# A fused retention and two-layer kernel on one core: plain outputs for units 5 to 7 and an earlier first block

## The chip, the core and the metric

The kernel runs on one core of a Trainium2 chip. A core has a matrix engine, TensorE (PE in the profile; PEld is its loading of stationary operands), and three engines that work on tiles: VectorE (DVE), ScalarE (ACT) and GpSimd (POOL). SyncE (SP) issues transfers; ACT and POOL can issue them too. Each engine works off its own instructions in the order in which they were written, and waits for the others through semaphores. The metric is the time of one execution on the device in microseconds (us); the kernel before takes 290.12 us, the median of 4 runs (289.74 to 290.54).

## What is computed

A retention layer (attention without a softmax, with a causal decay for each head) over 8 batches of 576 tokens, 8 heads of 64, and then two dense layers with a leaky rectifier between them on all 4608 tokens. Inputs and output are float32.

```python
scores = q @ k^T / sqrt(64)                          # per batch and head
gamma  = 1 - 2 ** (-5 - head)
ret    = scores * where(i >= j, gamma ** (i - j), 0)
x      = (ret @ v), heads side by side               # 4608 x 512
h      = x @ w_in                                    # 512 x 2048
g      = maximum(0.01 * h, h)
out    = g @ w_out                                   # 2048 x 512
```

## The kernel before

**Units and groups.** The tokens are cut into 36 units of 128, each of two chunks of 64, and into 9 groups of four units (512 tokens). Retention is done chunk by chunk with a running state, so a unit needs the state of the one before it. Units 0 to 3 make group 0, units 4 to 7 group 1.

**A unit's steps.** `load` brings k, q and v, 256 KB each. `cast_k` (ACT), `cast_q` and `cast_v` (L175, L179) make float16 copies, the latter two with a decay factor. q and k are transposed: in the beginning on PE (`turn_act`, `turn`: four matmuls into a PSUM tile and a copy to the tile qkT, L207), from unit 8 on by a transfer on the SP queue (`transpose_dma`, L183). `scores` (L218, L227) makes the products of q and k and the new state terms in one PSUM tile. `masks` (L236) applies the causal mask on DVE, `state` (L258 to L264) adds up the state on DVE, and `state_cast` (L279) gives it in float16.

**Two forms of a unit's outputs.** The part from inside the chunk (mask times v) and the part from the state have to be summed. `outputs` (L294, L305) writes the two parts to separate halves of a PSUM tile: 32 matmuls. Then `own` (L361) copies one half to SBUF on ACT, and `add` (L366) adds the other half to it on DVE, which gives the unit's columns of xT, the first layer's input. `finish2` is these three. `outputs_acc` (L327, L339) sums in PSUM: two rounds of 16 matmuls with a drain of PE between them; then ACT alone copies the sum to xT (`x_copy`, L347). `finish` is `outputs_acc`, `x_copy` and the cast of the unit's second state. `first_outputs` is the same form in another PSUM pool.

**First layer.** `h_half(g, a, fb)` does half a group's tokens (two units) for 256 of the 2048 columns: 8 matmuls 128x256 (L379), then the leaky rectifier on ACT (L393). `h_unit(u, fb)` does one unit's tokens for 512 columns in 16 matmuls 128x128. `h_block` does a whole group for 128 columns. A block needs the xT of its tokens and the quarter of w_in that holds its columns. All first-layer blocks, PE transposes and fillers take turns in the four PSUM tiles named acc. `keep_warm(n)` issues n matmuls on a tile of zeros whose result nobody reads.

**Second layer.** Group 0 uses plain products (`wide`, L429, 16 groups of four matmuls). The later groups use a scheme of seven block products instead of eight (`seven`, L493); it needs differences of blocks of w_out, made once on DVE (`mix_weights`, L454), and sums of blocks of g (`mix`, L473).

**The order.** Nothing is scheduled: the order on every engine is that of the program's lines. Lines 600 to 646 do units 0 to 3 with fillers between; lines 716 to 784 do units 4 to 7 between blocks of the first layer of groups 0 and 1; the loop at line 799 does the second layer of group 0, with `burst(u)` (scores, and the outputs of the unit before) of unit 8 after the fifth and of unit 9 after the tenth piece. Loads of units 0 to 7 and the weights go out on POOL's queue, save three at the start. The loads of units 8 to 10 and then the transposes of units 8 and 9 stand in that order on SP's queue; the first of these loads waits for the third of four w_out transfers (L762).

Of the kernel before, what the change touches and what calls it, by code (L numbers as in the profile page):

```python
# [18 lines left out]
def kernel(  # L19
# [9 lines left out]
    nc = tc.nc  # L29
# [54 lines left out]
    def behind(dma, *others):  # L84
        for o in others:
            tc.add_manual_dep(
                dma.ins,
                o.ins.name,
                mybir.DependencyInfo(
                    mybir.DependencyClass.Sync, mybir.DependencyReason.DATA  # L90
                ),
                reason="order of loads",
            )
# [20 lines left out]
    def half(i):  # L114
        return slice(CH * i, CH * i + CH)
# [3 lines left out]
    def load(u, eng=None, after=None):  # L119
        for x in (1, 0, 2):  # L120
            t = ld_pool.tile([P, H, D], FP, name=f"t32_{x}")
            t32[u, x] = t
            c = 2 * u
            same = c % CB + 1 < CB
            e = eng[x] if isinstance(eng, dict) else eng or nc.sync
            engs = e if isinstance(e, tuple) else (e,)
            n = H // len(engs)
            for j, rows in ((0, P),) if same else ((0, CH), (1, CH)):
                b, w = (c + j) // CB, (c + j) % CB
                for i, e in enumerate(engs):  # L130
                    hs = slice(n * i, n * i + n)
                    d = e.dma_start(
                        out=t[CH * j : CH * j + rows, hs],
                        in_=(q, k, v)[x][b, hs, CH * w : CH * w + rows, :].rearrange(
                            "h t d -> t h d"
                        ),
                    )
                    if after is not None and (x in after or not isinstance(after, dict)):
                        behind(d, *(after[x] if isinstance(after, dict) else after))
                        after = None  # L140
                    last_load[u, x] = d
# [24 lines left out]
    def decay(u, x):  # L166
        w = kinds.index((place(2 * u), place(2 * u + 1)))
        return tab_sb[:, w, x, :].unsqueeze(2).to_broadcast([P, H, D])
# [5 lines left out]
    def cast_q(u, eng):  # L174
        eng.tensor_tensor(out=qk16[u][:, 0], in0=t32[u, 0], in1=decay(u, 0), op=MUL)  # L175

    def cast_v(u, eng):
        v16[u] = a_pool.tile([P, H, D], F16, name="v16")
        eng.tensor_tensor(out=v16[u], in0=t32[u, 2], in1=decay(u, 1), op=MUL)  # L179
# [54 lines left out]
    def masks(u):  # L234
        s16s[u] = b_pool.tile([P, 2, NP, CH], F16, name="s16")
        nc.vector.tensor_tensor(  # L236
            out=s16s[u],
            in0=sc_tiles[u][:, :, 0],
            in1=mask_sb.unsqueeze(1).unsqueeze(1).to_broadcast([P, 2, NP, CH]),
            op=MUL,  # L240
        )
# [28 lines left out]
    def live(u, j):  # L270
        return (2 * u + j) % CB != CB - 1

    def state_cast(u, copy, js=(0, 1)):
        js = [j for j in js if live(u, j)]
        if len(js) == 2:
            copy(out=st16[u], in_=s32s[u])  # L276
        else:
            for j in js:
                copy(out=st16[u][:, j], in_=s32s[u][:, j])  # L279

    def st_before(u, j):
        if (2 * u + j) % CB == 0:
            return zst
        return st16[u][:, 0] if j else st16[u - 1][:, 1]

    def outputs(u):
        ot = ot_pool.tile([P, 2, 2 * NP, CH], FP, name="ot")
        ot_tiles[u] = ot
        far = ot[:, :, NP : 2 * NP].rearrange("q g (c j) t -> q g c j t", j=2)
        for c in range(NP):  # L290
            for j in range(2):
                for o in range(2):
                    h = c + NP * o
                    nc.tensor.matmul(  # L294
                        out=ot[half(o), j, c, :],
                        lhsT=v16[u][half(j), h, :],
                        rhs=s16s[u][half(j), h % 2, h // 2, :],
                        start=True, stop=True, skip_group_check=True,
                    )
        for j in range(2):  # L300
            for c2 in range(NP // 2):
                for o in range(2):
                    for g in range(2):
                        h = 2 * c2 + g + NP * o
                        nc.tensor.matmul(  # L305
                            out=far[half(o), g, c2, j, :],
                            lhsT=st_before(u, j)[half(g), h // 2, :],
                            rhs=qkT[u][half(g), 0, h // 2, half(j)],
                            start=True, stop=True, skip_group_check=True,
                        )  # L310
# [40 lines left out]
    def x_of(u):  # L351
        g, t0 = u // 4, (u % 4) * P
        if g not in xT:
            xT[g] = x_pool.tile([P, NP, TOK], F16, name="xT")
        return xT[g][:, :, t0 : t0 + P]
# [3 lines left out]
    def own(u):  # L359
        owns[u] = b_pool.tile([P, NP, 2, CH], FP, name="own")  # L360
        nc.scalar.copy(  # L361
            out=owns[u], in_=ot_tiles[u][:, :, 0:NP].rearrange("q j c t -> q c j t")
        )

    def add(u):
        nc.vector.tensor_tensor(  # L366
            out=x_of(u).rearrange("q (c g) t -> q c g t", g=2),
            in0=ot_tiles[u][:, :, NP : 2 * NP].rearrange("q g (c j) t -> q c g (j t)", j=2),
            in1=owns[u].rearrange("q (c g) j t -> q c g (j t)", g=2),
            op=ADD,  # L370
        )
# [5 lines left out]
    def h_mm(hps, n, g, f, ts):  # L377
        for c in range(NP):
            nc.tensor.matmul(  # L379
                out=hps[:, n, :],  # L380
                lhsT=w_in16[:, c, f * P : (f + 1) * P],
                rhs=xT[g][:, c, ts],
                start=(c == 0),
                stop=(c == NP - 1),
            )

    def g_tile(g):
        if g not in g_t:
            g_t[g] = g_pool.tile([P, NF, TOK], F16, name="gt")
        return g_t[g]  # L390

    def leaky(out, in_):
        nc.scalar.activation(out=out, in_=in_, func=mybir.ActivationFunctionType.Lrelu)  # L393
# [6 lines left out]
    def h_half(g, a, fb):  # L400
        ts = slice(a * HT, (a + 1) * HT)
        hps = acc_pool.tile([P, 2, HT], FP, name="acc")
        for n in range(2):
            h_mm(hps, n, g, 2 * fb + n, ts)
        leaky(g_tile(g)[:, 2 * fb : 2 * fb + 2, ts], hps)

    def h_unit(u, fb):
        g, t0 = u // 4, (u % 4) * P
        ts = slice(t0, t0 + P)
        hps = acc_pool.tile([P, 4, P], FP, name="acc")  # L410
        for n in range(4):
            h_mm(hps, n, g, 4 * fb + n, ts)
        leaky(g_tile(g)[:, 4 * fb : 4 * fb + 4, ts], hps)
# [142 lines left out]
    def keep_warm(n):  # L556
        t = acc_pool.tile([P, 1, TOK], FP, name="acc")
        for _ in range(n):
            nc.tensor.matmul(out=t[:, 0, :], lhsT=idle[:, 0:P], rhs=idle, start=True, stop=True)
# [6 lines left out]
    pool_copy, act_copy, dve_copy = nc.gpsimd.tensor_copy, nc.scalar.copy, nc.vector.tensor_copy  # L566
# [17 lines left out]
    def turn_act(u, x):  # L584
        transpose_pe(u, x)
        transposed(u, x, act_copy)
# [49 lines left out]
    cast_q(3, nc.vector)  # L636
    cast_v(3, nc.vector)
    turn_act(3, 0)
    keep_warm(2)
    masks(2)  # L640
    scores(3)
    state_last(2)
# [6 lines left out]
    def halves(g, *items):  # L649
        for a, fb in items:  # L650
            h_half(g, a, fb)

    def cast_qv(u):
        cast_q(u, nc.vector)
        cast_v(u, nc.vector)

    def turn(u, x):
        transpose_pe(u, x)
        transposed(u, x, dve_copy)

    def settle(u):
        state(u, 0)
        state_cast(u, dve_copy, (0,))
        masks(u)
        state(u, 1)

    def finish(u):
        outputs_acc(u)
        x_copy(u)
        state_cast(u, act_copy, (1,))  # L670

    def finish2(u):
        outputs(u)
        own(u)
        add(u)
# [37 lines left out]
        ahead(u + 2)  # L713


    halves(0, (0, 0), (0, 1))
    finish2(3)
    state_cast(3, act_copy, (1,))
    halves(0, (0, 2), (0, 3))
# [19 lines left out]
    scores(5)  # L739
    settle(5)  # L740
    cast_k(6)
    cast_qv(6)
    halves(0, (0, 6), (0, 7))
    finish(5)
    halves(0, (1, 6))
    turn(6, 1)
    cast_k(7)
    halves(0, (1, 7))
    turn(6, 0)
    cast_qv(7)  # L750
    h_unit(5, 0)
    scores(6)
    settle(6)
    h_unit(5, 1)
    turn(7, 1)
    halves(1, (0, 4))
    finish(6)
    turn(7, 0)
    halves(1, (0, 5))
    scores(7)  # L760
    settle(7)
    load(8, after=(w_out_loads[2],))  # L762
    load(9)
    halves(1, (0, 6), (0, 7))
    h_unit(6, 0)
    finish(7)
    h_unit(6, 1)
    mix_weights(0, 0)
    mix_weights(0, 1)
    h_unit(7, 0)  # L770
# [83 lines left out]
```

## Time and profile before

| what | value |
|---|---|
| median of 4 runs | 290.12 us (289.74 to 290.54) |
| profiled execution, its own time | 290.54 us |
| its span, first to last instruction | 288.8 us |
| busy time PE, DVE, ACT, POOL | 280.8, 170.1, 144.5, 103.6 us |
| granted clock of TensorE, mean | 1.000 |
| mean length of a DVE sum (L366), an ACT own copy (L361) | 682 ns, 586 ns |

The span is what the profile shows, and 1.7 us of the execution lie outside it. The stretch of the profile that the change touches runs from 16 to some 50 us. Times of instructions are given from the start of the span. A line of the timeline gives the start, the length, the engine, the line of the program, the operation, what it writes and reads, the shapes, the number of instructions merged in it, and in brackets how long its engine was idle ahead of it and what ended that. A matmul's end is modelled: the next one starts well before the end of the last.

### The profile page before, as it was taken

To read this page: it belongs to the slowest core of one execution; us is meant where nothing else is said; L and a number is where in the kernel's file an instruction comes from. 1 tells how busy PE (TensorE), PEld (TensorE's weight loads), DVE (VectorE), ACT (ScalarE), POOL (GpSimd) and SP (SyncE) were. 2 spreads that over 40 slices of the span, in tenths; PEclk is the share of its full clock that TensorE was granted. 3 is DMA by queue.
4 is the path that set the end of the run, shared out by engine and by line. 5 is a ranking of instruction groups with operands and counts; after the bars stand their busy time and mean duration, and the time that the engine had idled before them with its cause. 6 is when DMAs were issued, how large, how long until landed. Compare 5 with 4: busy or idle time off the path is not lost.

```text
span 288.8 us, 9437 instructions
## 1 busy us (share of the span) xinstructions
PE 280.8 (97%) x4113; PEld 191.6 (66%) x4113; DVE 170.1 (59%) x294; ACT 144.5 (50%) x254; POOL 103.6 (36%) x124
## 2 busy tenths in 40 slices
PE   8799999999999999999999999999999999999994
PEld 2468888645874587458745874587458844884584
DVE  2875668774663595359545863586268636840352
ACT  3766766633337732773277327731773176307610
POOL 8969502645433324332424333234225413000000
PEclk9999999999999999999999999999999999999999
DMA  8999999999999999966796669766986151012003
GB/s 218 295 231 203 289 207 205 192 176 223 176 255 278 226 205 223 265 147 148 176 260 152 148 148 288 149 147 150 279 162 147 42 179 39 5 62 86 0 2 145
DMA packets 131738, 50.01 MB, mean 173 GB/s; under 512 B 121264, under 2 KB 126000, under 8 KB 131696
## 3 DMA queue, kind: packets, MB, share of 16 engines
q1 hardware_dynamic: 125392, 39.59, 59.1%
q0 software_dynamic: 6016, 9.70, 15.1%
q8 instruction: 32, 0.52, 0.8%
q10 hardware_dynamic: 288, 0.11, 0.1%
q14 instruction: 10, 0.08, 0.1%
HBM read 36.81 MB, written 9.44 MB: 160 GB/s over the span
## 4 chain that ended last, share of the span: by engine, by line
PE 91%; DVE 4%; DMA 2%; issue 1%; ACT 1%; POOL 0%; DVEq 0%; POOLq 0%
PE acc L379 43%; PE acc L493 34%; PE acc L429 5%; PE sc L218 3%; DMA t<-in_q_dram 2%; PE ot L294 1%; PE sc L227 1%; PE ot L305 1%; PE acc L200 1%; DVE qk L175 1%; DVE s L236 1%; PE ot L327 1%; DVE st L279 1%; DVE s L260 1%; DVE v L179 0%
## 5 line engine op out<-in xcount | busy, mean ns | idle before, releaser
L379 PE MATMUL acc<-xT,w_in 128*128 128x512 f16 (+2 forms) x768 | 130.9, 326 | 0.0
L393 ACT ACTIVATE gt<-acc 128x512 f16<-128x512 f32 x144 | 85.9, 598 | 56.2 <-PE acc L379 54.5
L379 PEld LDWEIGHTS <-w_in 128*128 128x128 f16 x768 | 68.1, 98 | 51.3
L493 PEld LDWEIGHTS <-gt 128*128 128x128 f16 x640 | 61.8, 98 | 9.1
L236 DVE TENSOR_TENSOR s<-sc,cs 128x512 f16<-128x512 f32 x34 | 23.3, 685 | 40.0 <-PE sc L227 40.0
L493 PE MATMUL acc<-w_out,gt 128*128 128x256 f16 x384 | 45.9, 273 | 0.2
L276 POOL CAST st<-s 128x512 f16<-128x512 f32 x21 | 12.8, 611 | 89.7 <-DVE s L260 56.3
L361 ACT COPY own<-ot 128x512 f32<-128x512 f32 x30 | 17.6, 586 | 42.6 <-PE ot L305 34.4
L175 POOL TENSOR_TENSOR qk<-t,cs 128x512 f16<-128x512 f32 x28 | 30.0, 1071 | 19.8 <-ACT xT L347 15.2
L473 DVE TENSOR_TENSOR mix<-gt 128x1024 f16<-128x1024 f16 x16 | 14.8, 923 | 30.6 <-ACT gt L393 30.6
L179 POOL TENSOR_TENSOR v<-t,cs 128x512 f16<-128x512 f32 x28 | 31.3, 1117 | 1.7 <-DMA t<-in_v_dram 1.7
L493 PE MATMUL acc<-w_mix,gt 128*128 128x256 f16 x256 | 30.6, 273 | 0.0
L493 PE MATMUL acc<-w_mix,mix 128*128 128x256 f16 x256 | 29.6, 273 | 0.0
L493 PEld LDWEIGHTS <-mix 128*128 128x128 f16 x256 | 25.0, 98 | 3.1 <-DVE mix L473 0.2
L172 ACT CAST qk<-t 128x512 f16<-128x512 f32 x36 | 22.3, 620 | 5.8 <-DMA t<-in_k_dram 3.8
L366 DVE TENSOR_TENSOR xT<-ot,own 128x512 f16<-128x512 f32 x30 | 20.5, 682 | 3.8 <-ACT own L361 3.8
L260 DVE TENSOR_TENSOR s<-sc,s 128x256 f32<-128x256 f32 x37 | 15.5, 419 | 2.4 <-PE sc L227 1.7
L218 PEld LDWEIGHTS <-qkT 64*64 64x64 f16 x576 | 7.9, 107 | 12.4 <-issue 10.5
L519 DVE TENSOR_TENSOR osb<-acc,u 128x512 f32<-128x512 f32 (+1 forms) x17 | 11.2, 656 | 8.0 <-PE acc L493 8.0
L473 DVE TENSOR_TENSOR mix<-mix,gt 128x1024 f16<-128x1024 f16 x16 | 14.8, 932 | 0.5
L429 PE MATMUL acc<-w_out,gt 128*128 128x512 f16 x64 | 14.3, 379 | 0.0
L279 POOL CAST st<-s 128x256 f16<-128x256 f32 x7 | 3.2, 455 | 31.0 <-DVE s L264 19.1
(60 smaller groups left out, 240.0 us busy)
## 6 DMA issues: line engine op xcount, KB each, us to landing
out_dram<-osb SPq DMA_DIRECT2D x17, 512.0 KB, 4.0
t<-in_k_dram SPq DMA_DIRECT2D x27, 256.0 KB, 3.9
t<-in_q_dram SPq DMA_DIRECT2D x26, 256.0 KB, 4.4
t<-in_v_dram SPq DMA_DIRECT2D x25, 256.0 KB, 4.7
w_in<-in_moe_w_in_dram POOLq DMA_DIRECT2D x8, 256.0 KB, 6.9
w_out<-in_moe_w_out_dram POOLq DMA_DIRECT2D x4, 512.0 KB, 10.5
t<-in_v_dram POOLq DMA_DIRECT2D x7, 256.0 KB, 5.5
t<-in_q_dram POOLq DMA_DIRECT2D x6, 256.0 KB, 5.8
```

The source lines that it names most:

```text
L172: nc.scalar.copy(out=qk16[u][:, 1], in_=t32[u, 1])
L175: eng.tensor_tensor(out=qk16[u][:, 0], in0=t32[u, 0], in1=decay(u, 0), op=MUL)
L179: eng.tensor_tensor(out=v16[u], in0=t32[u, 2], in1=decay(u, 1), op=MUL)
L236: nc.vector.tensor_tensor(out=s16s[u], in0=sc_tiles[u][:, :, 0], in1=mask_sb.unsqueeze(1).unsqueeze(1).to_broadcast([P, 2, NP, CH]), op=MUL,)
L260: nc.vector.tensor_tensor(out=to, in0=st, in1=carry[0], op=ADD)
L361: nc.scalar.copy(out=owns[u], in_=ot_tiles[u][:, :, 0:NP].rearrange("q j c t -> q c j t"))
L366: nc.vector.tensor_tensor(out=x_of(u).rearrange("q (c g) t -> q c g t", g=2), in0=ot_tiles[u][:, :, NP : 2 * NP].rearrange("q g (c j) t -> ...
L379: nc.tensor.matmul(out=hps[:, n, :], lhsT=w_in16[:, c, f * P : (f + 1) * P], rhs=xT[g][:, c, ts], start=(c == 0), stop=(c == NP - 1),)
L393: nc.scalar.activation(out=out, in_=in_, func=mybir.ActivationFunctionType.Lrelu)
L429: nc.tensor.matmul(out=ys[tb], lhsT=g_t[0][:, f, tb * P : (tb + 1) * P], rhs=w_out16[:, f, :], start=(f == 0), stop=(f == NF - 1),)
L473: nc.vector.tensor_tensor(out=z[:, fs], in0=a[:, fs], in1=b[:, fs], op=op)
L493: nc.tensor.matmul(out=r[name][tb][:, 0, :] if apart else r[name][0][:, tb, :], lhsT=lhs[:, f, tb * P : (tb + 1) * P], rhs=rhs[:, f, :], s ...
```

## The change

- The first block of the first layer, `h_half(0, 0, 0)`, is issued where two fillers stood, between the q transpose of unit 3 and unit 2's masks, and is taken out of its old place ahead of unit 3's outputs. These therefore come one block sooner.
- Units 5, 6 and 7 use the plain outputs with the sum on DVE, where they had the form that sums in PSUM.
- For unit 5, the cast of v of unit 6 goes behind the sum. For unit 6, the casts of q and v of unit 7 go behind unit 6's masks and states, and the sum goes behind the q transpose's copy of unit 7. For unit 7, the outputs go behind both of unit 6's first-layer blocks, and two blocks of group 1 that stood ahead go behind unit 7's outputs.

```diff
@@ -636,7 +636,7 @@
     turn_act(3, 0)
-    keep_warm(2)
+    h_half(0, 0, 0)
     masks(2)
...
-    halves(0, (0, 0), (0, 1))
+    halves(0, (0, 1))
     finish2(3)
...
     cast_k(6)
-    cast_qv(6)
+    cast_q(6, nc.vector)
     halves(0, (0, 6), (0, 7))
-    finish(5)
+    finish2(5)
+    cast_v(6, nc.vector)
+    state_cast(5, act_copy, (1,))
     halves(0, (1, 6))
     turn(6, 1)
     cast_k(7)
     halves(0, (1, 7))
     turn(6, 0)
-    cast_qv(7)
     h_unit(5, 0)
     scores(6)
     settle(6)
+    cast_qv(7)
     h_unit(5, 1)
     turn(7, 1)
     halves(1, (0, 4))
-    finish(6)
+    outputs(6)
+    own(6)
     turn(7, 0)
+    add(6)
+    state_cast(6, act_copy, (1,))
     halves(1, (0, 5))
     scores(7)
     settle(7)
     load(8, after=(w_out_loads[2],))
     load(9)
+    h_unit(6, 0)
+    h_unit(6, 1)
+    finish2(7)
+    state_cast(7, act_copy, (1,))
     halves(1, (0, 6), (0, 7))
-    h_unit(6, 0)
-    finish(7)
-    h_unit(6, 1)
     mix_weights(0, 0)
```

No function is added or altered; both forms of the outputs stand in the kernel before.

## The prediction

> **What bounds the kernel now.** I read the page first, then the chain of work that ended last, then the timeline of each engine from 16 to 60 us, the DMA issues of that stretch, and the waits.
>
> ```profile
> PE 280.8 (97%) x4113; PEld 191.6 (66%) x4113; DVE 170.1 (59%) x294; ACT 144.5 (50%) x254; POOL 103.6 (36%) x124
> ...
> PE 91%; DVE 4%; DMA 2%; issue 1%; ACT 1%; POOL 0%; DVEq 0%; POOLq 0%
> ```
>
> TensorE (PE) is busy 97% of the span and makes 91% of the chain, so a microsecond taken from PE shows at the end only if nothing later makes PE wait for it. The change ends at about 49 us. What lies next on PE is in the chain (start, length, work):
>
> ```profile
> 48.26 6.28 PE acc L379 x80
> 54.54 4.32 PE acc L429 x20
> 58.86 0.25 PE sc L218 x16
> ```
>
> First-layer blocks, 20 matmuls of the second layer, then the scores of unit 8, with no gap. The timeline of the SP queue (start, length of the issue) and of PE around that place:
>
> ```profile
> 43.74 0.37 SPq L132 DMA_DIRECT2D t<-in_k_dram  x1
> ...
> 53.70 0.73 SPq L132 DMA_DIRECT2D t<-in_v_dram  x1
> 54.61 3.37 SPq L183 DMA_TRANSPOSE qkT<-qk  x2
> ...
> 58.79 0.21 PEld L218 LDWEIGHTS <-qkT 64*64 64x64 f16 x16 [0.42 <-DMA qkT<-qk]
> ```
>
> and the issues of the window that holds the first of the two transposes alone (us from issue to landing):
>
> ```profile
> qkT<-qk SPq DMA_TRANSPOSE x1, 4.1
> ```
>
> The transpose of unit 8 is issued at 54.61 and lands 4.1 us later, at 58.7. The scores of unit 8 need it and start at 58.79. So here PE and the DMA queue meet within 0.1 us: PE that comes earlier waits. What is ahead of the transpose in its queue is nine loads (units 8 to 10), and the first of them waited for a weight transfer, not for PE:
>
> ```profile
> SPq L132 <- DMA w_out<-in_moe_w_out_dram: 40.9, 1, 40.9
> ```
>
> **The change, part by part.** Sums are made on the profiled execution, 290.54 us with a span of 288.8; the median of the runs is 290.12, 0.42 lower, and I add my difference to that.
>
> *First block instead of two fillers.* The place on PE:
>
> ```profile
> 16.25 0.40 PE L200 MATMUL acc<-ident,qk 128*128 128x128 f16 x4 [0.29 <-DVE qk L175]
> 16.48 0.59 PE L559 MATMUL acc<-idle 128*128 128x512 f16 x2
> 17.32 0.32 PE L218 MATMUL sc<-qkT 64*64 64x64 f16 x16 [0.24 <-ACT qkT L207]
> ```
>
> The block needs xT of unit 1 (ScalarE (ACT) 15.99+0.59 = 16.58) and the second half of w_in's first quarter (issued 9.96, landing after 6.6: 16.56). So it starts at 16.64. Eight such matmuls with the hand-over to small ones take 0.97 (43.21 to 44.18, L379 then L218), so scores of unit 3 start at 17.61, 0.29 late. Further on, eight of sixteen matmuls are gone: 18.46 to 20.31 (1.85) becomes 0.97. Net -0.59 at unit 3's outputs (19.72, was 20.31). The mask they read ends at 18.50+0.68+0.29 = 19.47, in time. On ACT the block's leaky (0.60) now stands ahead of unit 2's state cast (17.76, becomes some 18.3), which is first read at 19.9: hidden by the 1.6 us between. If w_in is late, it is one for one on this gain. Nothing else there waits for a load: the tightest is v of unit 4, whose second half is issued at 16.84, lands 5.3 later at 22.14, and would be read at 22.73-0.59 = 22.14; the other loads and w_in quarters land a microsecond or more before their earlier use.
>
> *Plain outputs, unit 5.* The accumulating form holds PE from 35.40 to 36.29 (0.89, two halves with a drain between); the plain one from 20.31 to 20.69 and 28.71 to 29.09 (0.38): -0.51. Its sum costs VectorE (DVE) 0.69; ACT's copy is 0.58 for 0.59. From the plain rows, own starts 0.60 after the outputs and the sum 0.61 after own. Outputs at 34.82, so sum at 36.03, v of unit 6 behind it at 36.63, the two qkT copies at 37.23 and 37.67, done 38.09. PE comes to scores of unit 6 at 39.48-0.59-0.51 = 38.38: hidden, by 0.2 us.
>
> *Unit 6, with unit 7's casts behind unit 6's masks.* DVE starts that group 0.51 after the scores (33.17 to 33.68), 38.90, and needs 2.1 (40.24 to 42.36): q of unit 7 from 41.0 to 41.7. PE issues outputs at 40.87 (was 42.09, where it waited for the mask), and is at unit 7's q transpose at 41.25; it waits to 41.78, a new stall of 0.53. Copies follow v (41.6) at 42.23 and 42.67; scores of unit 7 at 43.15 (was 44.18). The sum of unit 6 stands behind the copies: 43.10 to 43.78. Scores end at 43.53, and the next block on PE, h_unit(6,0), now needs that sum: stall 0.31.
>
> *Unit 7, and two blocks moved behind it.* Same work from the scores' end to h_unit(7,0): 4.54 before (44.56 to 49.10), less 0.51, plus the 0.31: 47.87, was 49.10. Its sum ends at 47.6, hidden behind the two moved blocks (1.8). **PE is ahead by 1.23 us here**, and reaches scores of unit 8 at 57.56.
>
> *The weight differences on DVE* (L454) start at 47.6 instead of 46.29, behind the sum of unit 7, and so lie more beside GpSimd's (POOL's) casts:
>
> ```profile
> 47.49 1.28 DVE L454 TENSOR_TENSOR w_mix<-w_out,w_mix 128x1024 f16<-128x1024 f16 x2
> 48.70 2.13 DVE L454 TENSOR_TENSOR w_mix<-w_out 128x1024 f16<-128x1024 f16 x2
> ```
>
> A pair takes 1.28 alone and 2.13 beside the cast that starts at 48.91: 0.85 for one that meets one. Of the 1.3 us delay, the idle DVE had at 52.9 and 54.3 (0.72 and 1.05) takes 1.8; one or two more meetings cost 0.85 to 1.7. So DVE is between 0.5 early and 1.2 late at unit 8's mask (59.56). What waits for it, POOL's state cast at 61.09 and the outputs of unit 8 at 63.86, has 2 us to spare: nothing on the path. The Trainium skill ("SBUF — State Buffer", Who interferes with whom) speaks against this move: a DVE instruction with two SBUF inputs and a GpSimd one that reads SBUF exclude each other for a whole instruction. The rows agree in kind (2.13 for 1.28). By that rule all twelve such DVE instructions up to 59.6 could meet a cast, which would make DVE later than my bound; no row here has so many meetings.
>
> *The sum.* -1.23 as far as unit 8; there PE waits from 57.56 to 58.75: +1.2 back. The transpose does not move with PE: its queue starts at the landing of the third w_out part (32.26+11.4 = 43.67) and its nine loads then follow in order. The cast of k it also needs (ACT 52.45) and POOL's (to 51.7) are done by 54.6. Net 0: **290.1**. After 58.8 every instruction has its old time. The transfer itself can't be priced from the change; from below it is bounded by PE (at most -1.23), from above by the 1.0 us of the slower rival. I take 0, as the queue's input is the same. The Trainium skill ("DMA: Bandwidth & Descriptors", Anatomy of one DMA) gives a transfer some 2.0 us plus its bytes at 436 GB/s. For this one that would be an estimate of 2.6 us and a landing before PE arrives, and the sum would be the full gain; the row has 4.1, as it lies behind loads.
>
> **The rivals.**
> *The transpose lands earlier too, and the gain stays.* For it: the queue had a hole, 53.0 to 54.5, where one engine finished alone (an issue of 2.82 us at 50.78). In the window 50.2 to 52.2 one instruction packet took 5.9% of 16 engines, 1.9 us, while its kin at 44.4 took 1.0. If that is shorter when it comes at another moment, 0.9 us or more returns: 289.2, at best 290.12-1.23 = 288.9. Against: the packets come as often, and the queue works off the same bytes.
> *Slower: the queue starts later.* The instruction packet in the window from 44.4 to 45.5 (5.7% of 16 engines, 1.0 us) comes after the w_out part landed at 43.67. If it follows PE's progress, it comes 1.0 us sooner, about 43.4, and one of the sixteen engines holds up that landing, which all nine loads wait for. Price: up to 1.0, so 291.1; it decides when the first SP load is issued after 44.6. Against: 0.3 us of overlap is all there is, and the queue has slack at 46 to 47 us.
> *The change does not do what it says.* w_in's half lands 0.1 us before use, and the new stalls on DVE (0.53, 0.31) could be larger. With PE ahead by anything between 0 and 1.2 the time is the same 290.1; only a loss of over 1.2 shows.
>
> **How the numbers follow.** A measurement of this kernel tells 0.3% (0.87 us) from no change. Gain lost at unit 8, with the smaller-gain case: 0.56, 290.1, its own range 289.5 to 290.7. Transpose earlier by 0.9 or more: 0.27. Queue later, or new stalls beyond 1.2: 0.17. So faster 0.27, same 0.56, slower 0.17; the range goes to the full gain, 288.9, and to 291.0 above.
>
> **What would show it.** Block 0 on PE at 16.6, unit 3's outputs near 19.7, unit 6's at 40.9, unit 7's q transpose ended by DVE's cast, second-layer matmuls from 53.2, and a gap on PE of about 1.2 us before scores of unit 8, ended by the transpose at 58.7. Wrong: no gap there, or the first SP load off 43.7.

## The result, and the profile after

The changed kernel takes 289.66 us, the median of 52 runs (288.78 to 291.35). The kernel before takes 290.46 in 76 runs, not the 290.12 of the first four. The ratio is 0.9973, with a 95% interval of 0.9966 to 0.9981: 0.8 us faster. That is just inside the 0.3% that the prediction took for what can't be told from no change, but with so many runs it is clear of the noise. The predicted time, 290.1, held in this sense, and by luck: the wait that was to take the whole gain back is not there.

The profiled execution took 289.03 us, against 290.54 of the one before. From its page, the busy time of the engines and the shares of the chain of waits:

```profile
PE 278.9 (97%) x4111; PEld 190.2 (66%) x4111; DVE 172.8 (60%) x297; ACT 143.9 (50%) x254; POOL 104.1 (36%) x124
...
PE 90%; POOL 3%; DVE 3%; DMA 2%; issue 0%; POOLq 0%
```

PE is 1.9 us less busy, DVE 2.7 us more: three plain sums of 0.68 make 2.05 of this, and one more instruction of 1.53 for 0.68 beside POOL's casts most of the rest. The chain around unit 8 in the changed kernel (start, length, work):

```profile
45.98 7.13 PE acc L379 x80
53.12 4.32 PE acc L429 x20
57.43 0.25 PE sc L218 x16
```

Same pieces as before, 1.43 us sooner, and no gap ahead of the scores. Now PE's timeline in the same execution at five places:

```profile
16.75 1.03 PE L379 MATMUL acc<-xT,w_in 128*128 128x256 f16 x8 [0.23 <-DMA w_in<-in_moe_w_in_dram]
17.71 0.32 PE L218 MATMUL sc<-qkT 64*64 64x64 f16 x16
...
41.80 0.40 PE L200 MATMUL acc<-ident,qk 128*128 128x128 f16 x4 [0.39 <-DVE qk L175]
...
43.66 1.95 PE L379 MATMUL acc<-xT,w_in 128*128 128x128 f16 x32 [0.15 <-DVE xT L366]
...
57.36 0.32 PE L218 MATMUL sc<-qkT 64*64 64x64 f16 x16
```

The block waits for the second half of w_in's first quarter (the w_in half below), and the scores of unit 3 stand at 17.71 for 17.32 before. The q transpose of unit 7 waits for its cast, the next block for the sum of unit 6. The scores of unit 8 wait for nothing, and no gap on PE there was the prediction's own sign of being wrong. SP's queue was early too:

```profile
43.27 0.37 SPq L132 DMA_DIRECT2D t<-in_k_dram  x1
...
51.05 0.76 SPq L132 DMA_DIRECT2D t<-in_q_dram  x1
51.92 0.75 SPq L132 DMA_DIRECT2D t<-in_v_dram  x1
52.85 3.60 SPq L183 DMA_TRANSPOSE qkT<-qk  x2
```

Its first load goes out at 43.27 (43.74 before), the last load but one takes 0.76 to issue where it took 2.82, and the transpose is issued at 52.85 for 54.61. In a window from 52.5 to 55 the only transpose is the one of unit 8 (us to landing):

```profile
qkT<-qk SPq DMA_TRANSPOSE x1, 4.3
```

So it lands at 57.10, 1.6 us sooner than before and 0.26 ahead of PE. From the scores of unit 8 to the end it is 229.89 us, against 229.97 before. This one execution kept the whole lead; it is one of the fastest of the changed kernel, and the median of the runs kept 0.8 us. Where the other 0.6 goes is what the experiments ask.

### The profile page after: what moved, and what is told of

Same layout as the page of the kernel before. It is cut to its first block, busy times and chain, and to the rows that moved or that the text cites. A ratio compares the mean times of both kernels' runs of the same rounds, so it can differ in the third digit from the quotient of the medians.

```text
span 287.3 us, 9432 instructions
## 1 busy us (share of the span) xinstructions
PE 278.9 (97%) x4111; PEld 190.2 (66%) x4111; DVE 172.8 (60%) x297; ACT 143.9 (50%) x254; POOL 104.1 (36%) x124
## 4 chain that ended last, share of the span: by engine, by line
PE 90%; POOL 3%; DVE 3%; DMA 2%; issue 0%; POOLq 0%
PE acc L379 43%; PE acc L493 34%; PE acc L429 5%; POOL t L132 3%; PE sc L218 3%; DMA w_in<-in_moe_w_in_dram 2%; PE ot L294 2%; PE ot L305 1%; PE sc L227 1%; PE acc L200 0%; DVE s L236 0%; DVE xT L366 0%; DVE stmp L263 0%; DVE s L264 0%; DVE qkT L207 0%
## 5 line engine op out<-in xcount | busy, mean ns | idle before, releaser
L276 POOL CAST st<-s 128x512 f16<-128x512 f32 x21 | 12.8, 611 | 90.5 <-DVE s L260 56.3
L361 ACT COPY own<-ot 128x512 f32<-128x512 f32 x33 | 19.3, 585 | 42.8 <-PE ot L305 35.6
L473 DVE TENSOR_TENSOR mix<-gt 128x1024 f16<-128x1024 f16 x16 | 15.7, 983 | 28.8 <-ACT gt L393 28.8
L179 POOL TENSOR_TENSOR v<-t,cs 128x512 f16<-128x512 f32 x28 | 31.9, 1141 | 0.0
L366 DVE TENSOR_TENSOR xT<-ot,own 128x512 f16<-128x512 f32 x33 | 22.5, 682 | 5.1 <-ACT own L361 5.1
L473 DVE TENSOR_TENSOR mix<-mix,gt 128x1024 f16<-128x1024 f16 x16 | 13.1, 826 | 0.5
```

The costliest lines, as they stand in the source:

```text
L361: nc.scalar.copy(out=owns[u], in_=ot_tiles[u][:, :, 0:NP].rearrange("q j c t -> q c j t"))
L366: nc.vector.tensor_tensor(out=x_of(u).rearrange("q (c g) t -> q c g t", g=2), in0=ot_tiles[u][:, :, NP : 2 * NP].rearrange("q g (c j) t -> ...
L473: nc.vector.tensor_tensor(out=z[:, fs], in0=a[:, fs], in1=b[:, fs], op=op)
```

## The experiments

Each kernel was timed in five rounds beside the kernel before on the same chip; the medians of before were 290.3 to 290.4 us in all four groups. In seven of the twelve runs below the profiled execution is the slowest of its kernel, so a wait that is seen in it need not be one that the median met.

### Unit 8's transpose sooner or later, with the change and without

The edit of the first two lets unit 8's casts and transpose go ahead of the three loads of unit 10; that of the other two puts three more loads in front.

```diff
 # early
-    load(10)
     ahead(8)
+    load(10)
 # late
     load(10)
+    load(11)
     ahead(8)
...
     ahead(9)
-    load(11)
```

The changed kernel, early:

> The changed kernel with the transpose of unit 8 issued ahead of unit 10's three loads, so that it lands some 3 us before PE comes to unit 8's scores (about 54 us against 57.4). Theory T (the transpose's landing takes back part of the 1.4 us in most executions): the median falls to the fastest executions of the changed kernel, 288.8 to 289.1, and the spread shrinks to that of the kernel before (most within 0.4 us). Theory W (the late half of w_in's first quarter, which PE now waits for at 16.6, makes the spread): median and spread as in the changed kernel, 289.7 and 288.8 to 291.

The kernel before, early:

> The kernel before with the same early transpose. Theory T: no change, 290.4, ratio 1.000 within 0.1%, since PE comes at 58.8 when the transpose has mostly landed; only the executions over 291 become fewer. Theory W: no change either. If it were 0.2% faster or more, the transpose already held the kernel before, and part of a gain of the first run would not be the change's.

The changed kernel, late:

> The changed kernel with unit 11's three loads moved ahead of the transpose of unit 8, which so lands some 2.7 us later, at 59.8 to 61.4. Theory T: PE waits for it, the whole lead is lost and more: 291.2 to 292.8, and the time is that of the kernel before with the same edit, ratio between the two 1.000 within 0.2%. Theory W: the changed kernel keeps its lead of 0.3% over its twin.

The kernel before, late:

> The kernel before with unit 11's loads ahead of the transpose of unit 8. Theory T: 291.2 to 292.8, the same time as the changed kernel with this edit, as both wait for the same landing. Theory W: 0.3% slower than the changed kernel with this edit.

| kernel | median us (range) | ratio to before, 95% |
|---|---|---|
| changed, early | 289.32 (288.60 to 290.33) | 0.9961 (0.9937 to 0.9985) |
| before, early | 290.58 (290.06 to 292.13) | 1.0003 (0.9986 to 1.0020) |
| changed, late | 294.55 (292.98 to 296.06) | 1.0143 (1.0111 to 1.0175) |
| before, late | 292.58 (291.81 to 293.36) | 1.0074 (1.0054 to 1.0094) |

With the transpose out of the way the two kernels are 1.26 us apart, and 289.32 lies between the times of theory T (288.8 to 289.1) and theory W (289.7). With the transpose late they were to be level, as both would wait for the same landing; instead the changed kernel is 2.0 us the slower, and neither theory has that. The profile of the changed kernel is the slowest of its runs (296.06 us), that of the other one of the fastest (291.94). Of the 4.1 us between these two the landing makes 1.75, 61.97 against 60.22; the rest is on PE. The scores of unit 8, first in the changed kernel with the late transpose, then in the kernel before with it:

```profile
62.02 0.43 PE L218 MATMUL sc<-qkT 64*64 64x64 f16 x16 [4.04 <-DMA qkT<-qk]
```

```profile
60.27 0.32 PE L218 MATMUL sc<-qkT 64*64 64x64 f16 x16 [1.55 <-DMA qkT<-qk]
```

The windows of the former (stretch, its length, then busy time and count of PE, weight loads, DVE, ACT, POOL, then the granted clock, DMA share, GB/s):

```profile
58.00:60.00 2.00, 0.00 (x0) 0.00 (x0) 2.00 (x3) 0.62 (x1) 1.14 (x1) 1.00 1.09 241
60.00:62.00 2.00, 0.00 (x0) 0.00 (x0) 0.29 (x1) 0.00 (x0) 0.00 (x0) 0.55 1.23 211
62.00:64.00 2.00, 1.98 (x36) 1.09 (x37) 1.25 (x3) 0.00 (x0) 0.00 (x0) 0.50 0.80 179
64.00:66.00 2.00, 2.00 (x7) 0.63 (x6) 1.59 (x3) 0.00 (x0) 1.74 (x2) 0.50 1.06 241
66.00:68.00 2.00, 2.00 (x8) 0.83 (x7) 0.00 (x0) 0.43 (x1) 1.50 (x2) 0.74 0.80 180
```

PE has nothing from 58.0 to 62.0, and the granted clock is 0.5 from 60.21 to 67.04, long after PE has work again. From the scores of unit 8 to those of unit 9 takes 7.17 us where it took 4.80: 2.4 us lost. The wait of 1.55 us in the other kernel left the clock at 1.0. The recorded clocks of all runs say the same: a step of 3.41 us at half clock makes the mean granted clock 0.994, and the six runs of the changed kernel with the late transpose have 0.994 (four) or 0.988 (two, this one among them), the six of the kernel before with it 1.000. So PE's lead at a late transpose is not free: it lengthens the wait until the clock falls.

### The two parts of the change apart

```diff
 # the block alone, on the kernel before
     turn_act(3, 0)
-    keep_warm(2)
+    h_half(0, 0, 0)
...
-    halves(0, (0, 0), (0, 1))
+    halves(0, (0, 1))
 # the plain outputs alone: the changed kernel with these lines as before
```

The block alone:

> The kernel before with the first block alone in place of the two fillers. By the trace of the changed kernel unit 3's outputs come 0.47 us sooner when w_in's second half lands at 16.6. Theory T (the transpose of unit 8 takes gains back): PE comes to unit 8 at 58.3, so at most 0.1 to 0.5 is kept, 290.0 to 290.3, spread as before. Theory W (PE now waits for w_in itself, whose landing moves from one execution to the next): median 289.9 to 290.2 and the spread of the changed kernel, from 289.7 up past 291.

The plain outputs alone:

> The changed kernel with the two fillers and the block in their old places: the plain outputs alone. By the trace the lead is 1.43-0.47 = 0.96 us at unit 8. Theory W: all of it stays, 289.4 to 289.5, with the narrow spread of the kernel before. Theory T: PE comes at 57.8, a late transpose takes back up to 0.9, median 289.7 to 290.1 with a spread of 1 us and more.

The block alone gives 289.97 us (289.88 to 290.27), ratio 0.9987 (0.9971 to 1.0003); the plain outputs alone 289.45 (289.38 to 290.45), ratio 0.9971 (0.9955 to 0.9987). That is -0.36 and -0.88 us against 290.33; the first can't be told from nothing. The second is what theory W expects, with no transpose waited for (289.4 to 289.5), and not theory T (289.7 to 290.1). The fastest run with the block alone, 289.88, is no faster than the fastest of the kernel before in the same group, 289.71. In the profile of the block alone, PE at unit 3:

```profile
16.65 1.03 PE L379 MATMUL acc<-xT,w_in 128*128 128x256 f16 x8
...
19.74 0.32 PE L294 MATMUL ot<-s,v 64*64 64x64 f16 x16
```

Almost to the digit the working of the prediction (16.64 and 19.72). The profiled execution of the plain outputs alone is the slowest of its runs, 290.45 us; the scores of units 8 and 12 in it:

```profile
58.41 0.32 PE L218 MATMUL sc<-qkT 64*64 64x64 f16 x16 [0.55 <-DMA qkT<-qk]
...
80.06 0.32 PE L218 MATMUL sc<-qkT 64*64 64x64 f16 x16 [0.29 <-DMA qkT<-qk]
```

Here the predicted wait at unit 8 is to be seen, and a second one, not predicted, at unit 12. The one at unit 8 may start far ahead: this execution's half of w_in landed at 17.89, the third part of w_out at 44.51, the transpose at 58.36. In five profiles with the old order on SP's queue these are (landings, and the start of the scores of unit 8 on PE):

| profile | w_in half | third of w_out | transpose of unit 8 | PE at unit 8 |
|---|---|---|---|---|
| block alone | 16.33 | 43.09 | 56.25 | 58.22 |
| before | 16.55 | 43.67 | 58.69 | 58.79 |
| changed | 16.61 | 43.20 | 57.10 | 57.36 |
| changed, once more | 17.31 | 44.09 | 57.96 | 58.05 |
| plain outputs alone | 17.89 | 44.51 | 58.36 | 58.41 |

The w_in half is issued at 9.96 to 9.98 in each. The landing of the transpose has a scatter of 2.4 us and is not a fixed time, and the kernel before, with the latest of them but not the latest weights, shows that the weights are not all of it. PE without a wait comes between 57.4 and 58.8. In neither profile of the changed kernel did it wait there.

### An earlier cast of q of unit 7

The stall at 41.8 can go: the cast of q of unit 7 goes ahead of unit 6's masks, that of v behind them. It was run with the early transpose of unit 8, without the early block and with it.

```diff
-    settle(6)
-    cast_qv(7)
+    cast_q(7, nc.vector)
+    settle(6)
+    cast_v(7, nc.vector)
```

Without the block:

> The plain outputs alone, with the transpose of unit 8 ahead of unit 10's loads and with the cast of unit 7's q ahead of unit 6's masks, where DVE idles. The wait of PE's q transpose of unit 7 (0.39) goes, so the lead at unit 8 is about 1.3. Theory W: 289.0 to 289.2, narrow. Theory T: the same, as the transpose is out of the way; a spread that stays wide here falls to neither.

With the block:

> The changed kernel with the early transpose of unit 8 and the early cast of unit 7's q: lead 1.43+0.35 = 1.8 us in an execution whose w_in lands at 16.6. Theory W: fastest executions 288.3 to 288.6, median 288.7 to 289.2, spread 1.5 us and more. Theory T: median 288.6 to 288.8, narrow.

They take 288.93 us (288.32 to 290.12), ratio 0.9953 (0.9936 to 0.9970), and 288.47 (288.02 to 288.91), ratio 0.9925 (0.9900 to 0.9949). Both are a little below what was expected, the first with a spread of 1.8 us that falls to neither theory. From the scores of unit 3 to the block that waited at 43.66 it is 25.34 us in the profile with the block, and 25.95 in that of the changed kernel: 0.6 of the 0.85 between this kernel and the one with the early transpose alone. The profile of the kernel without the block is again its slowest execution; PE at units 12 and 15 in it:

```profile
79.24 0.32 PE L218 MATMUL sc<-qkT 64*64 64x64 f16 x16 [0.77 <-DMA qkT<-qk]
```

```profile
101.13 0.32 PE L218 MATMUL sc<-qkT 64*64 64x64 f16 x16 [0.52 <-DMA qkT<-qk]
```

The scores of unit 8 came at 57.10 without a wait, and 1.3 us went at the next two places. In the kernel before, the transposes of units 8, 12 and 15 land 0.1, 0.4 and 0.0 us before their scores; every other one up to unit 21 has 1.9 us or more. So PE can meet SP's queue at three places, not one. In the two profiles of the changed kernel it waits at none of them. Why unit 12 is tight shows on SP's queue, in the kernel with the block:

```profile
66.23 1.39 SPq L132 DMA_DIRECT2D t<-in_k_dram  x2
67.71 2.51 SPq L132 DMA_DIRECT2D t<-in_q_dram  x2
70.31 1.27 SPq L132 DMA_DIRECT2D t<-in_v_dram  x2
71.68 0.58 SPq L419 DMA_DIRECT2D out_dram<-osb  x1
72.43 1.69 SPq L183 DMA_TRANSPOSE qkT<-qk  x1
```

POOL's last cast for unit 12 is done at 68.5, but its transpose stands behind the loads of unit 13, in six halves, and goes out at 72.43.

### All three transposes ahead of their loads

```diff
     def step(u):
         burst(u)
-        fetch(u + 4)
         ahead(u + 2)
+        fetch(u + 4)
...
-        4: lambda: (burst(8, False), ahead(11), load(13)),
+        4: lambda: (burst(8, False), ahead(11)),
...
-        9: lambda: early(9, 12),
+        9: lambda: (burst(9), ahead(12), load(13), load(14)),
```

With the early transpose of unit 8 this was made to the kernel with the early cast, to the changed kernel, and to the kernel before; the changed kernel itself was run once more.

The changed kernel once more:

> The changed kernel once more, to set beside the kernel with the early transpose of unit 8 (289.32 us, ratio 0.9961) and as the measure for the run beside it. Theory M (lead of 1.2 to 1.4 us, taken back in part at whichever of the transposes of units 8, 12 and 15 lands late): 289.3 to 289.9 us, runs spread over more than 1 us, ratio about 0.997. Theory T8 (unit 8's transpose alone takes the lead back): the ratio is above that of the kernel with the early transpose by 0.002 or more.

With the early cast:

> The changed kernel with the early transpose of unit 8 and the early cast of q of unit 7 (288.47 us), and now the transpose of unit 12 issued ahead of unit 13's loads, and in the loop each transpose ahead of the loads of two units on. Theory M: unit 12's transpose is issued some 4 us sooner (68.5 to 69 for 72.4) and lands by 75, before PE comes at 78; unit 15's some 4 us sooner too; the waits of 0.29 us at unit 12 and of what was left at unit 15 are gone, and runs lie closer together: 288.0 to 288.3 us. Rival B (the transfers share bandwidth, so that order moves a landing by less than 1 us): 288.5, wait at unit 12 still there. Rival L (unit 13's loads, now behind, make its casts and its transpose late): a wait of 0.5 us or more ahead of the scores of unit 13, 289 us or more.

The changed kernel:

> The changed kernel with the transposes of units 8, 12 and 15 (and the loop's others) ahead of the loads they stood behind, cast of q of unit 7 as in the change. Theory M: no transpose is waited for any more, so the whole lead of 1.2 to 1.4 us stays: its median is below that of the kernel before with the same edit by 1.2 to 1.4 us; 288.9 to 289.2 us. Theory S (the lead is not lost at transposes but in the start, by late w_in and clock steps ahead of 20 us): below its twin by 0.9 us or less, with a wait for w_in in front of the first block, and as wide a spread as the changed kernel alone.

The kernel before:

> The kernel before with the same edit of the order on SP's queue. Theory M: it loses only its own small waits at units 8, 12 and 15 (0.1 us here and there): 290.1 to 290.3 us, ratio 0.999 to 1. A ratio under 0.998 would say that the transposes cost the kernel before as much as the changed one.

| kernel | median us (range) | ratio to before, 95% |
|---|---|---|
| changed, once more | 289.38 (288.91 to 289.73) | 0.9962 (0.9947 to 0.9976) |
| early cast, three transposes | 288.44 (287.97 to 289.46) | 0.9941 (0.9924 to 0.9958) |
| changed, three transposes | 289.00 (288.90 to 289.97) | 0.9952 (0.9933 to 0.9970) |
| before, three transposes | 290.43 (289.73 to 291.04) | 1.0002 (0.9988 to 1.0017) |

With no transpose in the way the median of the changed kernel is 1.43 us below its twin's, as much as the lead that the two first profiles show at unit 8 (58.79 and 57.36); the kernel before gains nothing by the same edit. That the edit brought the changed kernel its 0.6 us is not shown by this: its interval, 0.9933 to 0.9970, overlaps that of the changed kernel without it (0.9947 to 0.9976 in the run once more, 0.9966 to 0.9981 in the first result). Theory S, which puts the loss at the start, has the wrong price for the pair (0.9 us or less), but the runs are spread as it says, 288.90 to 289.97 against 288.91 to 289.73 once more. The scores of unit 8 stand at 58.26 and 58.89 in their profiles, neither with a wait. These are closer together than the medians, because the changed kernel's profile is its slowest execution and lost 0.9 us early. Its windows:

```profile
11.00:12.00 1.00, 0.92 (x26) 0.53 (x24) 0.86 (x4) 0.81 (x2) 1.00 (x3) 1.00 1.01 328
12.00:13.00 1.00, 0.44 (x11) 0.36 (x6) 1.00 (x2) 0.58 (x1) 1.00 (x2) 0.88 1.15 221
13.00:14.00 1.00, 1.00 (x8) 0.16 (x10) 1.00 (x3) 0.79 (x2) 1.00 (x3) 0.50 1.26 209
14.00:15.00 1.00, 1.00 (x38) 0.94 (x38) 0.86 (x3) 0.32 (x1) 0.85 (x2) 0.50 1.20 194
```

The clock falls to 0.5 for 3.4 us ahead of the place that the change touches, and the scores of unit 3 come at 18.62 for 17.71. Falls like this one don't make the 0.6 us of the median: such a step brings the mean clock to 0.994, and no recorded run of the changed kernel is under 0.997.

The kernel with the early cast misses its expectation of 288.0 to 288.3 and its narrow spread. The queue did what it should: the transpose of unit 12 is issued at 68.54 for 72.43 and the wait there is gone, and from unit 8 to the end it takes 229.89 us for 230.25. But the profiled execution, the slowest, lost more at the block:

```profile
17.79 1.03 PE L379 MATMUL acc<-xT,w_in 128*128 128x256 f16 x8 [1.21 <-DMA w_in<-in_moe_w_in_dram]
```

Here w_in's half landed at 17.66. Over all 14 profiles it landed between 15.94 and 17.89. In the kernel before its first reader came at 18.46, behind every one of these; the early block asks for it at some 16.5, in the middle of them.

The rerun, at 289.38, is level with the kernel that has unit 8's transpose early (289.32): that unit 8's place alone takes the lead back is not borne out. The profile of the rerun took 289.73 us, close to the median of the first result, and in it the scores of unit 3 stand at

```profile
18.41 0.32 PE L218 MATMUL sc<-qkT 64*64 64x64 f16 x16
```

0.69 us later than in the first profile of the changed kernel, and its half of w_in landed 0.69 us later (17.31 for 16.61). Set out this way, the profiles of the two kernels with the old order on SP's queue and with transposes early are:

| profile | its time | scores of unit 3 | from there to the end |
|---|---|---|---|
| before | 290.54 | 17.32 | 271.45 |
| before, early | 292.13 | 18.80 | 271.53 |
| before, three transposes | 290.55 | 17.42 | 271.36 |
| changed | 289.03 | 17.71 | 269.55 |
| changed, once more | 289.73 | 18.41 | 269.55 |
| changed, early | 289.96 | 18.63 | 269.53 |
| changed, three transposes | 289.97 | 18.62 | 269.55 |

Behind the scores of unit 3 the change is worth 1.8 to 2.0 us in every one, with the transposes early or not; what sets the executions of one kernel apart lies ahead of that place, by late w_in, the clock's step or an earlier delay. So in these profiles the lead is lost at the start and nothing of it at a transpose. Waits at transposes were seen only with the plain outputs alone, with the early cast and with the late transposes. Whether the runs that were not profiled, and with them the median's 0.6 us, follow the profiles is not shown.

## Why the prediction came out

*Block instead of two fillers: right, with a weak point that was named and not priced.* 16.75 and 19.84 for 16.64 and 19.72 in the changed kernel, 16.65 and 19.74 with the block alone. "If w_in is late, it is one for one": it is, by 0.2 to 1.2 us in the profiles, and I took one landing for a constant. In the rerun's profile, whose time is near the median, the landing and the block are both 0.69 us later than in the first, and nothing more is lost behind them.

*Plain outputs, unit 5: right.* Scores of unit 6 at 38.49 for 38.38, the same 0.1 late as the block.

*Unit 6 with unit 7's casts behind: right.* Outputs at 40.96 for 40.87, the q transpose at 41.80 for 41.78, scores of unit 7 at 43.06 for 43.15, the next block at 43.66 for 43.84. The early cast removes the first of the two stalls, for 0.6 us.

*Unit 7, lead at unit 8: mis-sized a little.* 1.43 for 1.23. The block after the stall came 0.2 sooner than worked out; the medians of the twins with the three transposes early are 1.43 apart as well.

*DVE's weight differences: right.* DVE's timeline in the changed kernel:

```profile
47.36 1.28 DVE L454 TENSOR_TENSOR w_mix<-w_out 128x1024 f16<-128x1024 f16 x2
48.56 2.98 DVE L454 TENSOR_TENSOR w_mix<-w_out,w_mix 128x1024 f16<-128x1024 f16 x2
...
59.67 0.68 DVE L236 TENSOR_TENSOR s<-sc,cs 128x512 f16<-128x512 f32 x1
```

The first pair was not slowed, the second one met a cast of POOL in each of its instructions (1.53 for 0.68). Of the twelve instructions up to unit 8's mask six were slowed so, and five before: one meeting more, of the one or two that I had allowed. The start is 1.07 later and the mask 0.11; idle time took up the rest, and nothing waited.

*PE waits from 57.56 to 58.75 for the transpose, net 0: this step failed, and that the time came out is luck here.* "The transpose does not move with PE: its queue starts at the landing of the third w_out part." The queue does start there (first load at 43.27, landing at 43.20), but the numbers were read off one execution and are not fixed. In the five profiles of the table that landing lies between 43.09 and 44.51, and from the first load's issue to the transpose's it takes 10.87 us in the profile of before, which I had read, and 9.41 to 9.71 in the others. So the transpose lands between 56.25 and 58.69, and I had read the latest. In the two profiles of the changed kernel it landed at 57.10 and 57.96, 0.26 and 0.09 us ahead of PE, and there was no wait. This is the rival of the early transpose. The instruction packet that it named took 1.89 us in the profile of before and 0.92 to 1.02 in the four others of the table, so its condition was met as well. The median kept 0.8 us, nearer to that rival's 0.9 than to my 0. The estimate of 2.6 us that I set aside rests on a formula that the skill's section gives for transfers issued from GpSimd, and this one is issued from SP; but in the seven profiles in which the transpose stands ahead of the three loads it lands 2.85 to 2.87 us after its issue, and in the five of the table, behind them, after 3.68 to 4.26. So the loads do make most of the difference.

*"After 58.8 every instruction has its old time": wrong, as it rests on the wait.* Everything behind it came 1.43 us sooner. I also followed the lead to the first meeting and no further: the transposes of units 12 and 15 were as tight as unit 8's in the trace of before (0.4 and 0.0 us of slack), and with the plain outputs alone and the early cast PE waited there.

*The slower rival, queue later by up to 1.0 us:* the first SP load goes out between 43.16 and 44.58 in the five profiles, at 43.27 and 44.16 in those of the changed kernel, and so never after the 44.6 that it named. For the median it was wrong. *That the change doesn't do what it says* is refuted by the first profile, with the lead of 1.43 us at unit 8.

*The median.* The sum started from four runs at 290.12, and 76 runs put the kernel before at 290.46. The measured 289.66 lies inside the range of 288.9 to 291.0. The gain of 0.80 stops 0.07 us short of the bound of 0.87, so "same" hung on the place of that bound and not on the reason given for it.

## What to carry to other kernels

Where an engine that sets the end meets a transfer within some tenths of a microsecond, list the slack of every such meeting down to the end of the kernel, not only of the next one; what a change gains can be lost again at whichever is tight. Moving the transfers ahead of loads that nobody waits for yet took these waits away here (unit 12: 0.29 us); that it also lowers the median is not shown. A landing read off one execution is one draw from a scatter that can be wider than the gain, and so is the execution's own start: compare profiles from a place behind it. Work moved forward to just behind a landing takes over that scatter: 0.59 us on paper came out as 0.36, and not told from nothing.

The fastest kernels here are the changed one with the early cast of q of unit 7 and the early transpose of unit 8, with or without the other two transposes: 288.47 and 288.44 us, ratios 0.9925 (0.9900 to 0.9949) and 0.9941 (0.9924 to 0.9958), below both the changed kernel and the one before.

## What the runs showed of the chip that was not expected

- A wait of 4.04 us on PE brought the granted clock to 0.5 2.2 us after PE had run out of work, and kept it there until 67.04, 5 us after PE had work again: two steps of 3.41 us, for 2.4 us lost. A wait of 1.55 us left it at 1.0. The Trainium skill ("TensorE: Matmul & The Clock Gate", Why this matters for your kernels) warns of PE gaps of more than about 3 us, and these two agree.
- The clock also fell to 0.5 for one step of 3.41 us, from 12.9 to 16.3 and from 12.8 to 16.2 us, in two of the 14 profiles (the changed kernel with one and with three transposes early), though PE had no gap of over 0.6 us in the step before. The scores of unit 3 came 0.9 us later in these two than in the first profile of the changed kernel. The same page's section What's actually happening ties the half clock to an idle window of 3.4 us, which these two rows don't show. What sets it off stays open.
- Transfers that are issued within 0.1 us of the same time land up to 2 us apart from execution to execution (the w_in half: 15.94 to 17.89 in 14 profiles).
- The transpose of unit 8 landed 2.85 to 2.87 us after its issue in the seven profiles in which it stood ahead of unit 10's loads, and 3.68 to 4.26 us after it in the five in which it stood right behind them.
